# Loading Wv by rows and entering the first two token tiles centred only, in the opening of a four-layer kernel

## Chip, cores, metric

One core of one Trainium2 chip. The metric is the device time of one execution in microseconds (us), median of several executions. The kernel before took 1295.47 us (3 runs, 1295.15 to 1295.88).

## The reference

The input is 2048 tokens of 1024 channels in bf16. Two kinds of layer alternate, twice each: dilated local attention, and an MLP that mixes tokens. Only the entry of the first attention layer matters here.

```python
x = x + A(layernorm(x), wqkv, wo)         # A: q, k, v = h @ wqkv ; local attention ; @ wo
x = x + B(layernorm(x), w1, b1, w2, b2)   # B: MLP over tokens
x = x + A(layernorm(x), wqkv, wo)
x = x + B(layernorm(x), w1, b1, w2, b2)
```

Layernorm is (x - mean) * rs with rs = 1 / sqrt(var + eps), one mean and one rs per token. The text calls the computation of rs the rsqrt; the kernel makes it of two small ScalarE operations, Ln and Exp. V is layernorm(x) @ Wv, and Wv is the last third of the columns of wqkv.

## The kernel before

Tokens come in 16 tiles of 128. In the opening each tile is loaded, gets its statistics and rs, is normalized and then transposed into hT, because the matmul wants channels on the partitions. Tiles 0 to 4 are transposed on TensorE into PSUM, the memory that holds matmul results, and copied to hT by ScalarE; the rest go by DMA transposes. To evict a result is to copy it out of PSUM, so that its buffer is free again. V of a tile is two output halves (n = 0, 1) of 512 columns, each a sum of eight matmuls over the eight blocks kt of 128 channels. Each engine works through a list of its own in the order written:

```python
def w_load(n, hf):      # 512 KB: one half of the columns of four kt, so rows of 1 KB
    return nc.sync.dma_start(out=wv[n][hf][:], in_=wq_v[:, hf*4:(hf+1)*4, 2*D + n*512:2*D + (n+1)*512])
def R_(k):  ...         # ScalarE: rs = Exp(-0.5 * Ln(var + eps))
def N_(k, hs): ...      # VectorE: x = (x - mean) * rs
def tr(k): ...          # TensorE: eight 128x128 transposes into PSUM
def C_(k, hf): ...      # ScalarE: four of them to hT
def V_(k, n, kts): ...  # TensorE: matmuls of tile k, half n, blocks kts
def E_(k, n):           # ScalarE: evict the finished half to v
    return nc.scalar.copy(out=v[c][i][:, n*512:(n+1)*512], in_=pss_[k, n][:])

for _ in range(14):     # warm matmuls on zeros, results unused: they are to get the clock fast
    chain_("PE", lambda: nc.tensor.matmul(wm[:], lhsT=warm[:, 0:P], rhs=warm[:], start=True, stop=True))
# ... cut ...
pe = [(tr, 0), (V_, 0, 0, lo4), (tr, 1), (V_, 0, 0, hi4), (V_, 1, 0, lo4), (tr, 2), (V_, 1, 0, hi4),
      (V_, 2, 0, a8), (V_, 0, 1, a8), (tr, 3), (V_, 1, 1, a8), (V_, 2, 1, a8), (tr, 4)]
pe += [(V_, k, n, a8) for k in range(3, NT) for n in range(NDC)]
act = [(R_, 0), (C_, 0, 0), (R_, 1), (C_, 0, 1), (C_, 1, 0), (C_, 1, 1), (R_, 2), (E_, 0, 0), (C_, 2, 0), (C_, 2, 1),
       (E_, 1, 0), (R_, 3), (E_, 2, 0), (R_, 4), (E_, 0, 1), (C_, 3, 0), ...]   # cut
```

The warm matmuls are there because the matmul clock starts slow: in this profile 512-column matmuls are issued every 0.427 us up to 7.3 us and every 0.216 us after that.

The softmax here doesn't subtract the row's maximum and nothing guards it: scores larger than these inputs give would overflow.

Of the kernel before, what the change touches and what calls it, by code (L numbers as in the profile page):

```python
# [14 lines left out]
P = 128  # L15
# [10 lines left out]
def kernel(  # L26
# [85 lines left out]
    def ln_exp_table():  # L112
        return tc.keep_in_program_order(nc.scalar.preload_act_table_set("natural_log_exp_and_others"))

    ln_exp_table()
    ident = const.tile([P, P], BF16, name="ident")
    make_identity(nc, ident[:])
    eps1 = const.tile([P, 1], FP32, name="eps1")
# [9 lines left out]
    for r in range(P // KG):  # L128
        hb_ = band[r * KG:(r + 1) * KG]
        nc.gpsimd.affine_select(out=hb_, in_=hb_, compare_op=ALU.is_ge, fill=0.0, base=0,  # L130
                                pattern=[[1, GW]], channel_multiplier=-1)
        nc.gpsimd.affine_select(out=hb_, in_=hb_, compare_op=ALU.is_ge, fill=0.0, base=W - 1,
                                pattern=[[-1, GW]], channel_multiplier=1)
    b1_bf = const.tile([P, FT], BF16, name="b1_bf")
    b2_bf = const.tile([P, NI, DIL], BF16, name="b2_bf")
    b1_sb = const.tile([P, FT], FP32, name="b1_sb")
# [48 lines left out]
        return mv[:, 0:1], rs  # L185

    def norm_dve(dst, x, mean, rs):
        return nc.vector.tensor_scalar(out=dst, in0=x, scalar1=mean, scalar2=rs[:], op0=ALU.subtract, op1=ALU.mult)

    def norm_act(dst, x, mean, rs):  # L190
        bi = st("bi", [P, 1])
# [11 lines left out]

    def start_up(v, wv):
        np_ = 5
        warm = x2("warm", [P, 512])
        nc.vector.memset(warm[:], 0.0)
        xs, tps, pss_, mvs, sts, rss = {}, {}, {}, {}, {}, {}

        def x_load(k, hs=(slice(0, D),)):  # L210
            c, i = order[k]
            if k % 2 == 0:
                x_load.t = gop.tile([P, GF, D], BF16, name="x0", tag="go")
            xs[k] = x_load.t[:, k % 2, :]
            for h in hs:
                r = nc.sync.dma_start(out=xs[k][:, h], in_=xin_v[c, i][:, h])
            return r

        def w_load(n, hf):
            return nc.sync.dma_start(out=wv[n][hf][:], in_=wq_v[:, hf * (KD // 2):(hf + 1) * (KD // 2),  # L220
                                                                2 * D + n * 512:2 * D + (n + 1) * 512])

        def S_(k, cc):
            if cc == 0:
                sts[k] = st("bn", [P, NDC, 6])
            return nc.vector.bn_stats(out=sts[k][:, cc, :], in_=xs[k][:, cc * 512:(cc + 1) * 512])

        def A_(k):
            mvs[k] = st("mv", [P, 2])
            return nc.vector.bn_aggr(out=mvs[k][:], in_=sts[k][:])  # L230

        def R_(k):
            rss[k] = st("rs", [P, 1])
            return rsqrt(rss[k][:], mvs[k][:, 1:2], 1.0, eps1)

        def N_(k, hs):
            for h in hs:
                r = norm_dve(xs[k][:, h], xs[k][:, h], mvs[k][:, 0:1], rss[k])
            return r

        def tr(k):
            tps[k] = pss.tile([P, KD, P], BF16, name="s", tag="s")
            for kt in range(KD):
                r = nc.tensor.transpose(tps[k][:, kt, :], xs[k][:, kt * P:(kt + 1) * P], ident[:])
            return r

        def C_(k, hf):
            ks = slice(hf * KD // 2, (hf + 1) * KD // 2)
            return nc.scalar.copy(out=hT[:, ks, cols(*order[k])], in_=tps[k][:, ks, :])  # L249

        def V_(k, n, kts):
            if kts[0] == 0:
                pss_[k, n] = m_tile()
            for kt in kts:
                r = nc.tensor.matmul(pss_[k, n][:], lhsT=hT[:, kt, cols(*order[k])], rhs=wv[n][kt // 4][:, kt % 4, :],  # L255
                                     start=(kt == 0), stop=(kt == KD - 1))
            return r

        def E_(k, n):
            c, i = order[k]  # L260
            return nc.scalar.copy(out=v[c][i][:, n * 512:(n + 1) * 512], in_=pss_[k, n][:])

        def T_(k):
            return nc.sync.dma_start_transpose(out=hT[:, :, cols(*order[k])], in_=xs[k])

        wm = m_tile()
        for _ in range(14):
            chain_("PE", lambda: nc.tensor.matmul(wm[:], lhsT=warm[:, 0:P], rhs=warm[:], start=True, stop=True))  # L268

        halves = (slice(0, D // 2), slice(D // 2, D))  # L270
        whole = (slice(0, D),)
        chain_("SP", x_load, 0, halves)
        chain_("SP", x_load, 1)
        chain_("SP", w_load, 0, 0)
        chain_("SP", x_load, 2)
        chain_("SP", w_load, 0, 1)
        chain_("SP", x_load, 3)
        chain_("SP", w_load, 1, 0)
        chain_("SP", w_load, 1, 1)
        for k in range(4, NT):  # L280
            chain_("SP", x_load, k)

        lo4, hi4 = range(KD // 2), range(KD // 2, KD)
        a8 = range(KD)
        pe = [(tr, 0), (V_, 0, 0, lo4), (tr, 1), (V_, 0, 0, hi4), (V_, 1, 0, lo4), (tr, 2), (V_, 1, 0, hi4),
              (V_, 2, 0, a8), (V_, 0, 1, a8), (tr, 3), (V_, 1, 1, a8), (V_, 2, 1, a8), (tr, 4)]
        pe += [(V_, k, n, a8) for k in range(3, NT) for n in range(NDC)]
        act = [(R_, 0), (C_, 0, 0), (R_, 1), (C_, 0, 1), (C_, 1, 0), (C_, 1, 1), (R_, 2), (E_, 0, 0), (C_, 2, 0), (C_, 2, 1),
               (E_, 1, 0), (R_, 3), (E_, 2, 0), (R_, 4), (E_, 0, 1), (C_, 3, 0), (C_, 3, 1), (R_, 5), (E_, 1, 1), (R_, 6),
               (E_, 2, 1), (C_, 4, 0), (C_, 4, 1)]  # L290
        es = [(E_, k, n) for k in range(3, NT) for n in range(NDC)]
        rs = [(R_, k) for k in range(7, NT)]
        for j, e in enumerate(es):
            act.append(e)
            if rs and j % 4 != 3:
                act.append(rs.pop(0))
        dve = [(S_, 0, 0), (S_, 0, 1), (A_, 0), (S_, 1, 0), (N_, 0, halves), (S_, 1, 1), (A_, 1), (N_, 1, whole),
               (S_, 2, 0), (S_, 2, 1), (A_, 2)]
        for k in range(2, NT):
            nx = k + 1 < NT  # L300
            if nx:
                dve.append((S_, k + 1, 0))
            dve.append((N_, k, whole))
            if nx:
                dve += [(S_, k + 1, 1), (A_, k + 1)]
        dve.append((zero_fill,))
        dve.append((cast_biases,))
        sp = [(T_, k) for k in range(np_, NT)] + [(load_biases,)]
        qs = {"PE": pe, "ACT": act, "DVE": dve, "SP": sp}
        need = {cast_biases: lambda: (load_biases,) in done, R_: lambda k: k in mvs, N_: lambda k, h: k in rss, tr: lambda k: (N_, k) in done, C_: lambda k, hf: k in tps,  # L310
                V_: lambda k, n, kts: ((C_, k, 1 if kts[-1] == KD - 1 else 0) in done or (T_, k) in done), E_: lambda k, n: (V_, k, n) in done,
                T_: lambda k: (N_, k) in done}
        done = set()
        while any(qs.values()):
            for eng, q in qs.items():
                while q and (q[0][0] not in need or need[q[0][0]](*q[0][1:])):
                    f, *args = q.pop(0)
                    chain_(eng, f, *args)
                    if f is V_:
                        if args[2][-1] == KD - 1:  # L320
                            done.add((f, args[0], args[1]))
                    else:
                        done.add((f, *(args if f is C_ else args[:1])))

    def load_wv():
        return [[wt_("wv", [P, KD // 2, 512]) for _ in range(2)] for _ in range(NDC)]

    def fill_wv(wv, n):
        for hf in range(2):
            nc.sync.dma_start(out=wv[n][hf][:],  # L330
                              in_=wq_v[:, hf * (KD // 2):(hf + 1) * (KD // 2), 2 * D + n * 512:2 * D + (n + 1) * 512])

    def v_proj(v, c, i, wv, ns):
        for n in ns:
            ps = m_tile()
            for kt in range(KD):
                nc.tensor.matmul(ps[:], lhsT=hT[:, kt, cols(c, i)], rhs=wv[n][kt // 4][:, kt % 4, :],  # L337
                                 start=(kt == 0), stop=(kt == KD - 1))
            nc.scalar.copy(out=v[c][i][:, n * 512:(n + 1) * 512], in_=ps[:])

# [242 lines left out]
    def gemm2(c, i, w2t, g, src, dst, to_hT):  # L583
# [17 lines left out]
            nc.sync.dma_start(out=dst, in_=xo[:])  # L601
        if to_hT:
            mean, rs = stats(xo, 1.0, eps1)
            norm_dve(xs[:], xo[:], mean, rs)
            nc.sync.dma_start_transpose(out=hT[:, :, cols(c, i)], in_=xs[:])

    NU = NG * DIL
    for li in range(2):
# [8 lines left out]
            chain_("SP", load_qk, 0, wts)  # L617
            res = lambda c, i: xin_v[c, i]
        else:
            fill_wv(wv, 0)  # L620
            fill_wv(wv, 1)
            wts = [None, None]
            chain_("SP", load_qk, 0, wts)
            for i in range(NI):
# [107 lines left out]
```

## Time and profile before

| | kernel before |
|---|---|
| median, 3 runs | 1295.47 us |
| span of the profiled execution | 1293.7 us |
| TensorE busy | 1276.5 us (99%) |
| first transpose of tile 0 | 7.32 us |
| first V matmul of tile 0 | 8.61 us |
| first V matmul of tile 3 | 21.54 us |
| first q matmul (all of V issued) | 66.43 us |

Two lines of the page: each engine's busy time in us, its share of the span and its number of instructions; and the shares of the chain of work that ended last.

```profile
PE 1276.5 (99%) x8286; PEld 593.7 (46%) x8442; DVE 417.3 (32%) x852; ACT 373.2 (29%) x628; POOL 2.4 (0%) x15
...
PE 98%; issue 1%; DVE 0%; DMA 0%; ACT 0%; SPq 0%
```

TensorE bounds everything. The Trainium skill warns ("Perfetto Trace Analysis", its opening note) that busy time of pipelined matmuls says little about distance from the peak. It does here only because the issue times agree: from 21.54 us to the first q matmul, and in the MLP stages, 512-column matmuls are issued every 0.216 us without a break, so this change can move the end only if TensorE reaches that stretch earlier.

The timeline of the opening, TensorE only (start, length, engine, line, operation, number of instructions, and in brackets idle time before and what ended it; a few matmul records are missing from a trace, so that x19 stands for 20). L268 are the warm matmuls, L244 the transposes, L255 the V matmuls:

```profile
1.38 6.11 PE L268 MATMUL m<-warm 128*128 128x512 bf16 x14 [1.38 <-DVE warm L207]
7.32 0.61 PE L244 MATMUL s<-ident,x 128*128 128x128 bf16 x8
8.61 1.04 PE L255 MATMUL m<-wv,hT 128*128 128x512 bf16 x4 [0.68 <-ACT hT L249]
9.62 0.62 PE L244 MATMUL s<-ident,x 128*128 128x128 bf16 x8
10.08 1.89 PE L255 MATMUL m<-wv,hT 128*128 128x512 bf16 x8
12.42 0.62 PE L244 MATMUL s<-ident,x 128*128 128x128 bf16 x8 [0.45 <-DVE x L188]
13.09 4.26 PE L255 MATMUL m<-wv,hT 128*128 128x512 bf16 x19
17.19 0.61 PE L244 MATMUL s<-ident,x 128*128 128x128 bf16 x8
17.64 3.62 PE L255 MATMUL m<-wv,hT 128*128 128x512 bf16 x16
21.09 0.61 PE L244 MATMUL s<-ident,x 128*128 128x128 bf16 x8
```

After tile 0 starts, only the transposes of tile 2 (12.42) are waited for noticeably. From the full timeline, Ln, Exp and the normalization of tile 0:

```profile
4.80 0.29 ACT L174 ACTIVATE ln<-mv,eps 128x1 f32<-128x1 f32 x1 [2.72 <-DVE mv L230]
5.12 0.20 ACT L175 ACTIVATE rs<-ln 128x1 f32<-128x1 f32 x1
5.37 0.73 DVE L188 TENSOR_SCALAR x<-x,mv,rs 128x512 bf16<-128x512 bf16 x2
```

### The profile page before, as it was taken

How to read it: one execution, taken by the hardware profiler on the slowest of the kernel's cores; microseconds unless marked ns; L12 is line 12 of the kernel's file. 1: busy time of each engine (PE TensorE's matmuls, PEld its weight loads, DVE VectorE, ACT ScalarE, POOL GpSimd, SP SyncE). 2: the span in 40 equal slices, each digit the busy share in tenths (PEclk: the TensorE clock that was granted, in tenths of full speed). 3: DMA queues.
4: the chain of work that ended last, by engine and by line, in shares of the span. 5: the costliest groups of instructions: out<-in, count | busy, mean ns of one | idle time of the engine just before them, and what ended most of it. 6: DMA issues, size and time to landing. Idle time of an engine off the chain costs nothing.

```text
span 1293.7 us, 19400 instructions
## 1 busy us (share of the span) xinstructions
PE 1276.5 (99%) x8286; PEld 593.7 (46%) x8442; DVE 417.3 (32%) x852; ACT 373.2 (29%) x628; POOL 2.4 (0%) x15
## 2 busy tenths in 40 slices
PE   9999999999999999999999999999999999999999
PEld 4444444444444444444444444444444444444444
DVE  7457767830000022322300667778100000111111
ACT  5456665541111100000023666644311111000000
POOL 0000000000000000000000000000000000000000
PEclk9999999999999999999999999999999999999999
DMA  7411123643222135456510111246422222334331
GB/s 236 82 44 48 51 80 122 204 138 90 65 78 80 57 101 148 124 155 147 130 33 1 46 51 49 80 151 209 125 66 86 78 59 78 105 106 135 118 92 33
DMA packets 201862, 125.54 MB, mean 97 GB/s; under 512 B 39984, under 2 KB 183600, under 8 KB 201776
## 3 DMA queue, kind: packets, MB, share of 16 engines
q1 hardware_dynamic: 201776, 124.30, 33.9%
q8 instruction: 66, 1.08, 0.3%
q14 instruction: 20, 0.16, 0.0%
HBM read 96.48 MB, written 16.78 MB: 88 GB/s over the span
## 4 chain that ended last, share of the span: by engine, by line
PE 98%; issue 1%; DVE 0%; DMA 0%; ACT 0%; SPq 0%
PE m L352 17%; PE s L594 15%; PE s L547 15%; PE m L467 8%; PE acc L547 7%; PE m L547 7%; PE acc L594 7%; PE m L594 7%; PE m L337 4%; PE m L255 4%; PE s L383 2%; PE acc L418 1%; PE acc L422 1%; PE m L268 0%; DMA qB<-qs 0%
## 5 line engine op out<-in xcount | busy, mean ns | idle before, releaser
L594 PEld LDWEIGHTS <-w 128*128 128x128 bf16 x1820 | 177.0, 98 | 210.2
L547 PEld LDWEIGHTS <-w 128*128 128x128 bf16 x1792 | 175.4, 98 | 211.4
L352 PE MATMUL m<-hT,wqk 128*128 128x512 bf16 x963 | 223.3, 379 | 6.2 <-issue 4.6
L547 PE MATMUL s<-h,w 128*128 128x512 bf16 x878 | 201.2, 379 | 0.8
L594 PE MATMUL s<-g,w 128*128 128x512 bf16 (+1 forms) x912 | 201.0, 374 | 0.7
L596 DVE SCALAR_TENSOR_TENSOR xo<-s,b_sb,xs 128x512 bf16<-128x512 f32 (+1 forms) x33 | 24.4, 739 | 532.9 <-PE s L594 527.6
L352 PEld LDWEIGHTS <-wqk 128*128 128x128 bf16 x1024 | 95.3, 98 | 117.9 <-issue 10.7
L398 DVE TENSOR_TENSOR Pm<-pc,band 32x640 bf16<-32x640 bf16 x256 | 123.5, 483 | 66.0 <-ACT pc L386 56.6
L467 PE MATMUL m<-wo,oT 128*128 128x512 bf16 x500 | 110.6, 379 | 0.8 <-issue 0.3
L547 PE MATMUL acc<-h,w 128*128 128x512 bf16 x440 | 103.1, 379 | 0.5
L594 PE MATMUL acc<-g,w 128*128 128x512 bf16 x436 | 99.7, 379 | 0.5
L547 PE MATMUL m<-h,w 128*128 128x512 bf16 x438 | 98.5, 379 | 0.5
L594 PE MATMUL m<-g,w 128*128 128x512 bf16 (+1 forms) x436 | 96.9, 376 | 0.6
L174 ACT ACTIVATE ln<-mv,eps 128x1 f32<-128x1 f32 x64 | 18.9, 295 | 221.1 <-DVE mv L182 184.9
L467 PEld LDWEIGHTS <-oT 128*128 128x128 bf16 x512 | 49.6, 98 | 60.3 <-issue 1.3
L554 ACT ACTIVATE g<-s,b_sb 128x1024 bf16<-128x1024 f32 x28 | 31.2, 1114 | 158.2 <-PE s L547 146.5
L363 DVE COPY qB<-qs 32x512 bf16<-32x512 bf16 x136 | 38.1, 280 | 90.5 <-ACT qs L359 89.2
L255 PE MATMUL m<-wv,hT 128*128 128x512 bf16 x250 | 55.6, 379 | 1.0 <-ACT hT L249 0.7
L337 PE MATMUL m<-wv,hT 128*128 128x512 bf16 x251 | 55.2, 379 | 0.3
L386 ACT ACTIVATE pc<-s,shift 128x640 bf16<-128x640 f32 x64 | 51.2, 800 | 12.2 <-PE s L383 12.1
L359 ACT CAST qs<-m 128x512 bf16<-128x512 f32 x64 | 37.5, 586 | 49.1 <-PE m L352 48.0
L356 ACT CAST kT<-m 128x512 bf16<-128x512 f32 x64 | 37.5, 586 | 46.4 <-PE m L352 46.4
(58 smaller groups left out, 675.1 us busy)
## 6 DMA issues: line engine op xcount, KB each, us to landing
w<-in_B_w_dram SPq DMA_DIRECT2D x56, 512.0 KB, 3.8
w<-in_B_w_dram SPq DMA_DIRECT2D x64, 448.0 KB, 4.5
wqk<-in_A_wqkv_dram SPq DMA_DIRECT2D x16, 512.0 KB, 4.8
xa<-xn SPq DMA_DIRECT2D x32, 256.0 KB, 2.2
xs<-xa SPq DMA_DIRECT2D x32, 256.0 KB, 3.1
wv<-in_A_wqkv_dram SPq DMA_DIRECT2D x8, 512.0 KB, 5.7
wo<-in_A_wo_dram SPq DMA_DIRECT2D x8, 512.0 KB, 6.0
xr<-in_A_x_dram SPq DMA_DIRECT2D x16, 256.0 KB, 3.3
```

Source lines behind the costliest of these rows:

```text
L255: r = nc.tensor.matmul(pss_[k, n][:], lhsT=hT[:, kt, cols(*order[k])], rhs=wv[n][kt // 4][:, kt % 4, :], start=(kt == 0), stop=(kt == KD - 1))
L337: nc.tensor.matmul(ps[:], lhsT=hT[:, kt, cols(c, i)], rhs=wv[n][kt // 4][:, kt % 4, :], start=(kt == 0), stop=(kt == KD - 1))
L352: mm = nc.tensor.matmul(ps[:], lhsT=wts[part][:, kt, (g % 2) * P:(g % 2 + 1) * P], rhs=hT[:, kt, lo:lo + 512], start=(kt == 0), stop=(kt = ...
L356: nc.scalar.copy(out=kT[u % 2][:, ls], in_=ps[:])
L359: nc.scalar.copy(out=qs[:], in_=ps[:])
L363: nc.vector.tensor_copy(out=qB[u % 2][hp, h, ls], in_=qs[hp, :])
L386: nc.scalar.activation(out=pc[:].rearrange("p (n t) h k -> p n (t h k)", n=2), in_=ss[:, :, 0:2 * HG * GW], func=ACT.Exp, scale=scale, bia ...
L398: mm = nc.vector.tensor_tensor(out=Pm[rp, :, s0:s0 + HB, r * KG:r * KG + GW].rearrange("p h t k -> p t h k"), in0=pc[rp], in1=mk, op=ALU.mult)
L467: mm = nc.tensor.matmul(ps[:], lhsT=oT[g][:, cols(c, i)], rhs=wo[n][g // 4][:, g % 4, :], start=(g == 0), stop=(g == NG - 1))
L547: nc.tensor.matmul(pairs[fl][0][dc], lhsT=wt[c][:, i, fl * P:(fl + 1) * P], rhs=h2[c][i][:, dc * 512:(dc + 1) * 512], start=(k == 0), stop ...
L554: nc.scalar.activation(out=g[fb][:, fl, :].rearrange("p (n d) -> p n d", n=2), in_=t[:], func=ACT.Gelu_apprx_tanh, bias=b1_sb[:, ft:ft + 1])
L594: nc.tensor.matmul(ap, lhsT=w2t[ft // HF][:, ft % HF, c::DIL], rhs=g[ft // GF][:, ft % GF, lo:lo + w], start=(ft == 0), stop=(ft == FT - 1))
```

## The change

The intent: reach V sooner. Tiles 0 and 1 enter hT centred only (x - mean), so they need not wait for rs; rs is applied when V is evicted. Wv comes as eight chunks of 256 KB with full 2 KB rows, and each chunk serves both output halves of both tiles. Because q and k need the normalized tiles, tiles 0 and 1 are normalized and DMA-transposed into hT a second time later. There are 10 warm matmuls, then 2 more behind the first transposes. The core of the diff, the rest cut:

```diff
-        def w_load(n, hf):
-            return nc.sync.dma_start(out=wv[n][hf][:], in_=wq_v[:, hf * (KD // 2):(hf + 1) * (KD // 2),
-                                                                2 * D + n * 512:2 * D + (n + 1) * 512])
+        def w_load(kt):
+            return nc.sync.dma_start(out=wv[kt // 2][:, kt % 2, :], in_=wq_v[:, kt, 2 * D:3 * D])
+        def M_(k, h):     # VectorE: centre
+            return nc.vector.tensor_scalar(out=xc[k][:, h], in0=xs[k][:, h], scalar1=mvs[k][:, 0:1], scalar2=None,
+                                           op0=ALU.subtract)
+        def Ma(k, h):     # ScalarE: centre
+            return nc.scalar.activation(out=xc[k][:, h], in_=xs[k][:, h], func=ACT.Identity, bias=nm0[:])
 # E_:
+            if k < 2:
+                return nc.scalar.activation(out=dst, in_=src, func=ACT.Identity, scale=rss[k])
-        for _ in range(14):
+        for _ in range(10):
 # loads: Wv 0 to 3, x of tile 2, Wv 4 and 5, x of tile 3, Wv 6 and 7
+        pe = [(tr, 0), (W_, 2), *VV(0, 0, 1), (tr, 1), *VV(0, 2), *VV(1, 0, 1, 2)]
+        for kt in range(3, 6):
+            pe += [*VV(0, kt), *VV(1, kt)]
+        pe += [(tr, 2), *VV(0, 6, 7), *VV(1, 6, 7), (V_, 2, 0, a8), (tr, 3), (V_, 2, 1, a8), (tr, 4)]
+        act = [(Ma, 0, halves[1]), (C_, 0, 0), (C_, 0, 1), (R_, 0), (C_, 1, 0), (C_, 1, 1), (R_, 1), (R_, 2), (C_, 2, 0), (C_, 2, 1),
+               (E_, 0, 0), (E_, 0, 1), (E_, 1, 0), (E_, 1, 1), (R_, 3), (R_, 4), (C_, 3, 0), (C_, 3, 1), (E_, 2, 0),
+               (R_, 5), (C_, 4, 0), (C_, 4, 1), (E_, 2, 1), (R_, 6)]
+            if k in (8, 9):
+                dve.append((N_, k - 8, whole))
-        sp = [(T_, k) for k in range(np_, NT)] + [(load_biases,)]
+        sp = [(T_, k) for k in (*range(np_, NT), 0, 1)] + [(load_biases,)]
```

VV(k, kt) is one matmul of tile k for each output half. In the second attention layer Wv is also loaded by rows; nothing else there changes.

More of the change, by code (lines that the diff above doesn't have):

```diff
@@ L113, in ln_exp_table @@
         return tc.keep_in_program_order(nc.scalar.preload_act_table_set("natural_log_exp_and_others"))
-    ln_exp_table()
     ident = const.tile([P, P], BF16, name="ident")
@@ L133 @@
                                 pattern=[[-1, GW]], channel_multiplier=1)
+    mv01 = const.tile([P, 2, 2], FP32, name="mv01")
+    rs01 = const.tile([P, 2], FP32, name="rs01")
+    nm0 = const.tile([P, 1], FP32, name="nm0")
     b1_bf = const.tile([P, FT], BF16, name="b1_bf")
@@ L187, in norm_dve @@
     def norm_dve(dst, x, mean, rs):
-        return nc.vector.tensor_scalar(out=dst, in0=x, scalar1=mean, scalar2=rs[:], op0=ALU.subtract, op1=ALU.mult)
+        return nc.vector.tensor_scalar(out=dst, in0=x, scalar1=mean, scalar2=rs, op0=ALU.subtract, op1=ALU.mult)
     def norm_act(dst, x, mean, rs):
@@ L205, in start_up @@
         np_ = 5
+        xc = [x2(f"xc{k}") for k in range(2)]
         warm = x2("warm", [P, 512])
@@ L228, in A_, with B_ @@
         def A_(k):
-            mvs[k] = st("mv", [P, 2])
-            return nc.vector.bn_aggr(out=mvs[k][:], in_=sts[k][:])
+            mvs[k] = mv01[:, k, :] if k < 2 else st("mv", [P, 2])[:]
+            return nc.vector.bn_aggr(out=mvs[k], in_=sts[k][:])
+        def B_(k):
+            return nc.vector.tensor_scalar(out=nm0[:], in0=mvs[k][:, 0:1], scalar1=-1.0, scalar2=None, op0=ALU.mult)
+        def M_(k, h):
[3 more added lines that the diff above has]
+            return nc.scalar.activation(out=xc[k][:, h], in_=xs[k][:, h], func=ACT.Identity, bias=nm0[:])
         def R_(k):
-            rss[k] = st("rs", [P, 1])
-            return rsqrt(rss[k][:], mvs[k][:, 1:2], 1.0, eps1)
+            rss[k] = rs01[:, k:k + 1] if k < 2 else st("rs", [P, 1])[:]
+            return rsqrt(rss[k], mvs[k][:, 1:2], 1.0, eps1)
         def N_(k, hs):
@@ L243, in tr @@
             for kt in range(KD):
-                r = nc.tensor.transpose(tps[k][:, kt, :], xs[k][:, kt * P:(kt + 1) * P], ident[:])
+                r = nc.tensor.transpose(tps[k][:, kt, :], (xc[k] if k < 2 else xs[k])[:, kt * P:(kt + 1) * P], ident[:])
             return r
@@ L251, in V_ @@
         def V_(k, n, kts):
-            if kts[0] == 0:
-                pss_[k, n] = m_tile()
+            if kts[0] == 0 and k == 1:
+                if n == 0:
+                    V_.t = a_tile()
+                pss_[k, n] = V_.t[:, n, :]
+            elif kts[0] == 0:
+                pss_[k, n] = m_tile()[:]
             for kt in kts:
-                r = nc.tensor.matmul(pss_[k, n][:], lhsT=hT[:, kt, cols(*order[k])], rhs=wv[n][kt // 4][:, kt % 4, :],
+                r = nc.tensor.matmul(pss_[k, n], lhsT=hT[:, kt, cols(*order[k])], rhs=wv[kt // 2][:, kt % 2, n * 512:(n + 1) * 512],
                                      start=(kt == 0), stop=(kt == KD - 1))
@@ L260, in E_ @@
             c, i = order[k]
-            return nc.scalar.copy(out=v[c][i][:, n * 512:(n + 1) * 512], in_=pss_[k, n][:])
+            dst, src = v[c][i][:, n * 512:(n + 1) * 512], pss_[k, n]
+            if k < 2:
+                return nc.scalar.activation(out=dst, in_=src, func=ACT.Identity, scale=rss[k])
+            return nc.scalar.copy(out=dst, in_=src)
         def T_(k):
             return nc.sync.dma_start_transpose(out=hT[:, :, cols(*order[k])], in_=xs[k])
-        wm = m_tile()
-        for _ in range(14):
-            chain_("PE", lambda: nc.tensor.matmul(wm[:], lhsT=warm[:, 0:P], rhs=warm[:], start=True, stop=True))
+        wm = s_tile()
@@ L270, in start_up, with W_ @@
+        def W_(n):
+            for _ in range(n):
+                r = nc.tensor.matmul(wm[:, 0, :], lhsT=warm[:, 0:P], rhs=warm[:], start=True, stop=True)
+            return r
+        for _ in range(10):
+            chain_("PE", W_, 1)
         halves = (slice(0, D // 2), slice(D // 2, D))
         whole = (slice(0, D),)
+        chain_("ACT", ln_exp_table)
         chain_("SP", x_load, 0, halves)
         chain_("SP", x_load, 1)
-        chain_("SP", w_load, 0, 0)
+        for kt in range(4):
+            chain_("SP", w_load, kt)
@@ L275, in start_up, with VV @@
         chain_("SP", x_load, 2)
-        chain_("SP", w_load, 0, 1)
+        chain_("SP", w_load, 4)
+        chain_("SP", w_load, 5)
         chain_("SP", x_load, 3)
-        chain_("SP", w_load, 1, 0)
-        chain_("SP", w_load, 1, 1)
+        chain_("SP", w_load, 6)
+        chain_("SP", w_load, 7)
         for k in range(4, NT):
             chain_("SP", x_load, k)
-        lo4, hi4 = range(KD // 2), range(KD // 2, KD)
+        def VV(k, *kts):
+            return [(V_, k, n, [kt]) for kt in kts for n in range(NDC)]
@@ L284, in start_up @@
         a8 = range(KD)
-        pe = [(tr, 0), (V_, 0, 0, lo4), (tr, 1), (V_, 0, 0, hi4), (V_, 1, 0, lo4), (tr, 2), (V_, 1, 0, hi4),
-              (V_, 2, 0, a8), (V_, 0, 1, a8), (tr, 3), (V_, 1, 1, a8), (V_, 2, 1, a8), (tr, 4)]
+        pe = [(tr, 0), (W_, 2), *VV(0, 0, 1), (tr, 1), *VV(0, 2), *VV(1, 0, 1, 2)]
+        for kt in range(3, 6):
+            pe += [*VV(0, kt), *VV(1, kt)]
+        pe += [(tr, 2), *VV(0, 6, 7), *VV(1, 6, 7), (V_, 2, 0, a8), (tr, 3), (V_, 2, 1, a8), (tr, 4)]
         pe += [(V_, k, n, a8) for k in range(3, NT) for n in range(NDC)]
-        act = [(R_, 0), (C_, 0, 0), (R_, 1), (C_, 0, 1), (C_, 1, 0), (C_, 1, 1), (R_, 2), (E_, 0, 0), (C_, 2, 0), (C_, 2, 1),
-               (E_, 1, 0), (R_, 3), (E_, 2, 0), (R_, 4), (E_, 0, 1), (C_, 3, 0), (C_, 3, 1), (R_, 5), (E_, 1, 1), (R_, 6),
-               (E_, 2, 1), (C_, 4, 0), (C_, 4, 1)]
+        act = [(Ma, 0, halves[1]), (C_, 0, 0), (C_, 0, 1), (R_, 0), (C_, 1, 0), (C_, 1, 1), (R_, 1), (R_, 2), (C_, 2, 0), (C_, 2, 1),
+               (E_, 0, 0), (E_, 0, 1), (E_, 1, 0), (E_, 1, 1), (R_, 3), (R_, 4), (C_, 3, 0), (C_, 3, 1), (E_, 2, 0),
+               (R_, 5), (C_, 4, 0), (C_, 4, 1), (E_, 2, 1), (R_, 6)]
@@ L296, in start_up @@
                 act.append(rs.pop(0))
-        dve = [(S_, 0, 0), (S_, 0, 1), (A_, 0), (S_, 1, 0), (N_, 0, halves), (S_, 1, 1), (A_, 1), (N_, 1, whole),
+        dve = [(S_, 0, 0), (S_, 0, 1), (A_, 0), (B_, 0), (M_, 0, halves[0]), (S_, 1, 0), (S_, 1, 1), (A_, 1), (M_, 1, whole[0]),
                (S_, 2, 0), (S_, 2, 1), (A_, 2)]
@@ L305, in start_up @@
                 dve += [(S_, k + 1, 1), (A_, k + 1)]
+            if k in (8, 9):
+                dve.append((N_, k - 8, whole))
         dve.append((zero_fill,))
         dve.append((cast_biases,))
-        sp = [(T_, k) for k in range(np_, NT)] + [(load_biases,)]
+        sp = [(T_, k) for k in (*range(np_, NT), 0, 1)] + [(load_biases,)]
         qs = {"PE": pe, "ACT": act, "DVE": dve, "SP": sp}
-        need = {cast_biases: lambda: (load_biases,) in done, R_: lambda k: k in mvs, N_: lambda k, h: k in rss, tr: lambda k: (N_, k) in done, C_: lambda k, hf: k in tps,
-                V_: lambda k, n, kts: ((C_, k, 1 if kts[-1] == KD - 1 else 0) in done or (T_, k) in done), E_: lambda k, n: (V_, k, n) in done,
-                T_: lambda k: (N_, k) in done}
+        need = {cast_biases: lambda: (load_biases,) in done, R_: lambda k: k in mvs, N_: lambda k, h: k in rss, tr: lambda k: (N_, k) in done if k > 1 else (M_, k) in done and (k == 1 or (Ma, k) in done),
+                B_: lambda k: k in mvs, M_: lambda k, h: k in mvs, Ma: lambda k, h: (B_, k) in done, C_: lambda k, hf: k in tps,
+                V_: lambda k, n, kts: ((C_, k, kts[-1] * 2 // KD) in done or (T_, k) in done), E_: lambda k, n: (V_, k, n) in done and k in rss,
+                T_: lambda k: (N_, k) in done and (k > 1 or (E_, k, 1) in done)}
         done = set()
@@ L322, in start_up, with fill_wv @@
                     else:
-                        done.add((f, *(args if f is C_ else args[:1])))
+                        done.add((f, *(args if f in (C_, E_) else args[:1])))
     def load_wv():
-        return [[wt_("wv", [P, KD // 2, 512]) for _ in range(2)] for _ in range(NDC)]
-    def fill_wv(wv, n):
-        for hf in range(2):
-            nc.sync.dma_start(out=wv[n][hf][:],
-                              in_=wq_v[:, hf * (KD // 2):(hf + 1) * (KD // 2), 2 * D + n * 512:2 * D + (n + 1) * 512])
+        return [wt_("wv", [P, 2, D]) for _ in range(KD // 2)]
+    def fill_wv(wv):
+        for j in range(KD // 2):
+            nc.sync.dma_start(out=wv[j][:], in_=wq_v[:, 2 * j:2 * j + 2, 2 * D:3 * D])
     def v_proj(v, c, i, wv, ns):
@@ L336, in v_proj @@
             for kt in range(KD):
-                nc.tensor.matmul(ps[:], lhsT=hT[:, kt, cols(c, i)], rhs=wv[n][kt // 4][:, kt % 4, :],
+                nc.tensor.matmul(ps[:], lhsT=hT[:, kt, cols(c, i)], rhs=wv[kt // 2][:, kt % 2, n * 512:(n + 1) * 512],
                                  start=(kt == 0), stop=(kt == KD - 1))
@@ L603, in gemm2 @@
             mean, rs = stats(xo, 1.0, eps1)
-            norm_dve(xs[:], xo[:], mean, rs)
+            norm_dve(xs[:], xo[:], mean, rs[:])
             nc.sync.dma_start_transpose(out=hT[:, :, cols(c, i)], in_=xs[:])
@@ L619 @@
         else:
-            fill_wv(wv, 0)
-            fill_wv(wv, 1)
+            fill_wv(wv)
             wts = [None, None]
```

## The prediction

> **What bounds the kernel.** TensorE. The busy table gives PE 1276.5 of 1293.7 us; the chain that ended last is 98% PE. After 21.5 us the matmuls run back to back at 0.216 us to the end, so the change acts only through the time at which PE reaches that stretch: in the timeline, the first V matmul of tile 3 at 21.54 us. Before it PE does 14 warm matmuls, then from 7.32 us 13.4 us of needed work (40 transposes, 48 matmuls) with gaps of 0.7 (first copy to hT), 0.3 and 0.45 to 0.8 us (normalized tile 2). At most some 2 us of gaps plus an earlier start are to be won.
>
> **What the change does, with the timeline's durations.**
> - The first transposes no longer wait for Ln and Exp (0.29 + 0.20) and two normalizing halves (0.73). The aggregate ends at 4.77; the centring halves run in parallel on DVE (0.37) and ACT (0.59), to about 5.6. Ten warm matmuls end at 1.38 + 10 x 0.427 = 5.65: transposes start near 5.65, not 7.32.
> - The clock is then still cold: matmuls are 0.427 apart until 7.32, 0.216 after. The Trainium skill, "TensorE: Matmul & The Clock Gate", Part 1, says about 3.4 us of sustained activity, judged in a free-running window, warms it; the trace shows 5.9 us. Eight cold transposes (0.85 estimated) and two warm matmuls (0.85) bring V of tile 0 to 7.4, not 8.61.
> - Wv: with queues full, a 512 KB chunk of 1 KB rows took 1.49 us, 256 KB of 2 KB rows 0.67. The eight chunks should land between 5.9 and 12.4 us, ahead of use. ("DMA: Bandwidth & Descriptors", Specifications, puts line rate at 512 B and up; the trace shows 12% between 1 and 2 KB.) PE didn't wait for weights and won't.
> - Tile 1's copy costs about 0.4 us of wait; transposes of tile 2 come near 13.4.
> - Given back: ACT now does two copies, then four evictions of tiles 0 and 1 in a row (0.48 each, issue to issue) before the rsqrt of tile 3. I estimate that rsqrt at 17.0, its normalize at 17.5, transposes at 18.1, while PE finishes V of tile 2, first half, at 17.4: 0.7 us idle. The rsqrt of tile 4 waits in turn for DVE (18.9); its transposes end near 20.7, then two waits of 0.3 for evictions. V of tile 3 starts near 21.0; at V of tile 4 the gain is about 0.2 us.
> - Two normalizations (0.55 each) and two DMA transposes (2 us each) are added behind; q/k weights are issued 4 us later (about 52.5, landing near 58.5). PE needs them at 66.4: no cost.
> - Second layer: Wv lands 15 us before use. Nothing.
>
> So 1.2 us gained at the start are nearly all given back on ACT before tile 4.
>
> **Predicted time** 1295.2 us, 8 in 10 between 1294.2 and 1296.2. Faster by over 2%: 0.01; within 2%: 0.98; slower: 0.01.
>
> **What would show it.** Timeline: transposes of tile 0 at 5.6 to 5.8; V of tile 0 at 7.2 to 7.6; no PE wait for wv; PE idle 0.5 to 1.2 us before the transposes of tile 3, released by its normalize; V of tile 3 at 20.5 to 21.5; first q matmul at 66.0 to 66.6 (66.4 before).
>
> **What would make it wrong.** The clock warming earlier or later (0.5 us either way); ACT overlapping better, so that tile 3 is not late (gain up to 1.5 us); wv chunks landing late (loss of 1 us); the last transposes landing after 66 us (loss of some us).

## The result, and the profile after

| | before | after |
|---|---|---|
| median of 6 runs, same rounds | 1295.28 us | 1295.82 us |
| lowest to highest | 1294.65 to 1295.88 | 1294.93 to 1296.29 |
| ratio, 95% interval | | 1.0004 (0.9991 to 1.0017) |
| first transpose of tile 0 (one profile each) | 7.32 us | 5.62 us |
| first V matmul of tile 0 | 8.61 us | 7.36 us |
| first V matmul of tile 3 | 21.54 us | 21.37 us |
| first q matmul | 66.43 us | 66.61 us |
| from V of tile 0 to first q, "the stretch" | 57.82 us | 59.25 us |

A ratio is the mean time of one kernel's runs over that of the other's runs of the same rounds, so it is not quite the ratio of the medians.

The time did not move. The same two lines of the page, after:

```profile
PE 1276.2 (99%) x8284; PEld 593.7 (46%) x8440; DVE 417.8 (32%) x854; ACT 373.5 (29%) x629; POOL 2.4 (0%) x15
...
PE 97%; issue 1%; ACT 1%; DVE 0%; DMA 0%; SPq 0%
```

ScalarE has entered the chain with 1%. Where, the timeline of TensorE says (L289 warm matmuls, L256 transposes, L271 V):

```profile
1.38 4.45 PE L289 MATMUL s<-warm 128*128 128x512 bf16 x10 [1.38 <-DVE warm L210]
5.62 1.06 PE L256 MATMUL s<-ident,xc 128*128 128x128 bf16 x8
6.48 0.77 PE L289 MATMUL s<-warm 128*128 128x512 bf16 x2
7.36 1.04 PE L271 MATMUL m<-wv,hT 128*128 128x512 bf16 x4
8.23 0.61 PE L256 MATMUL s<-ident,xc 128*128 128x128 bf16 x8
8.68 0.59 PE L271 MATMUL m<-wv,hT 128*128 128x512 bf16 x2
9.52 1.47 PE L271 MATMUL acc<-wv,hT 128*128 128x512 bf16 x6 [0.25 <-ACT hT L261]
...
13.42 0.61 PE L256 MATMUL s<-ident,x 128*128 128x128 bf16 x8
...
15.78 1.89 PE L271 MATMUL m<-wv,hT 128*128 128x512 bf16 x8
18.52 0.62 PE L256 MATMUL s<-ident,x 128*128 128x128 bf16 x8 [0.85 <-DVE x L190]
18.97 1.89 PE L271 MATMUL m<-wv,hT 128*128 128x512 bf16 x8
20.70 0.61 PE L256 MATMUL s<-ident,x 128*128 128x128 bf16 x8
21.37 5.82 PE L271 MATMUL m<-wv,hT 128*128 128x512 bf16 x24
```

The head start of 1.25 us (8.61 - 7.36) is there. What V of tile 0 waited for is not printed, but ScalarE's line shows it (two copies, of which the first ends near 7.31):

```profile
6.72 1.07 ACT L261 COPY hT<-s 128x512 bf16<-128x512 bf16 x2 [1.05 <-PE s L256]
```

Further on, tile 2 is transposed at 13.42, with most of V of tiles 0 and 1 done. Then TensorE stops before the transposes of tile 3 (18.52). Issue to issue it is 1.01 us without work: the last matmul before them was issued at 17.29 and the next could have gone out 0.216 us later. Summed from the issue times, the gaps between V of tile 0 and V of tile 4 are 2.10 us after and 0.75 us before; the 1.35 us between them are nearly all of the 1.43 us by which the stretch grew.

The bracket names the normalization of tile 3 on VectorE as what ended the wait. That was waiting in turn. From the full timeline of the changed kernel, ScalarE (L261 copies to hT, L279 scaled evictions, L176 and L177 Ln and Exp) and VectorE (L190):

```profile
14.06 1.07 ACT L261 COPY hT<-s 128x512 bf16<-128x512 bf16 x2 [2.32 <-PE s L256]
15.03 1.28 ACT L279 ACTIVATE v<-m,rs 128x512 bf16<-128x512 f32 x2
16.18 1.29 ACT L279 ACTIVATE v<-acc,rs 128x512 bf16<-128x512 f32 x2
17.32 0.33 ACT L176 ACTIVATE ln<-mv,eps 128x1 f32<-128x1 f32 x1
17.68 0.20 ACT L177 ACTIVATE rs<-ln 128x1 f32<-128x1 f32 x1
17.91 0.55 DVE L190 TENSOR_SCALAR x<-x,mv,rs 128x1024 bf16<-128x1024 bf16 x1 [3.63 <-ACT rs L177]
```

The statistics of tile 3 were ready at 13.56 us, while ScalarE had been idle for 2.32 us until 14.06. Its list, however, puts six large operations before the rsqrt of tile 3, so that came at 17.32 and VectorE idled for 3.63 us.

### The profile page after: what moved, and what is told of

It reads as the page before. It is cut to its first block, busy times and chain, and to the rows that moved or that the text cites. A ratio compares the mean times of both kernels' runs of the same rounds, so it can differ in the third digit from the quotient of the medians.

```text
span 1293.7 us, 19408 instructions
## 1 busy us (share of the span) xinstructions
PE 1276.2 (99%) x8284; PEld 593.7 (46%) x8440; DVE 417.8 (32%) x854; ACT 373.5 (29%) x629; POOL 2.4 (0%) x15
## 3 DMA queue, kind: packets, MB, share of 16 engines
q8 instruction: 66, 1.08, 0.4%
## 4 chain that ended last, share of the span: by engine, by line
PE 97%; issue 1%; ACT 1%; DVE 0%; DMA 0%; SPq 0%
PE m L386 17%; PE s L628 15%; PE s L581 15%; PE m L501 8%; PE acc L581 7%; PE m L581 7%; PE acc L628 7%; PE m L628 7%; PE m L371 4%; PE m L271 4%; PE s L417 2%; PE acc L452 1%; PE acc L456 1%; PE s L289 0%; ACT hT L261 0%
## 5 line engine op out<-in xcount | busy, mean ns | idle before, releaser
L176 ACT ACTIVATE ln<-mv,eps 128x1 f32<-128x1 f32 x64 | 18.9, 296 | 224.1 <-DVE mv L184 184.9
L371 PE MATMUL m<-wv,hT 128*128 128x512 bf16 x251 | 55.2, 379 | 0.3
L271 PE MATMUL m<-wv,hT 128*128 128x512 bf16 x234 | 53.0, 379 | 0.6
```

The costliest lines, as they stand in the source:

```text
L271: r = nc.tensor.matmul(pss_[k, n], lhsT=hT[:, kt, cols(*order[k])], rhs=wv[kt // 2][:, kt % 2, n * 512:(n + 1) * 512], start=(kt == 0), st ...
L371: nc.tensor.matmul(ps[:], lhsT=hT[:, kt, cols(c, i)], rhs=wv[kt // 2][:, kt % 2, n * 512:(n + 1) * 512], start=(kt == 0), stop=(kt == KD - 1))
```

## The experiments

Theory A: the head start is real and is lost on ScalarE, because the rsqrt of tile 3 stands behind the evictions of tiles 0 and 1. Rival B: it is lost because x of tiles 2 and 3 lands later behind the Wv chunks (9.62 and 11.54 us, against 7.75 and 10.01). Rival C: the second entry of tiles 0 and 1 costs time. Theory D, on the head start itself: before, the start was held by the 14 warm matmuls, and centring is worth little.

The executions differ by 1 to 2 us for reasons shown below, as much as is at stake. So each kernel is judged first by its trace: the stretch from V of tile 0 to the first q matmul. All runs, with the moment at which the matmul clock turned fast (from an issue spacing of 0.427 to 0.216 us, worked out from the spacing of the matmul during which it turned):

| kernel | clock fast at, us | V tile 0 | first q | stretch | median, us | ratio to before, interval |
|---|---|---|---|---|---|---|
| before | 7.3 | 8.61 | 66.43 | 57.82 | 1295.28 | 1 |
| before, again | 6.1 | 8.03 | 65.85 | 57.82 | 1295.29 | 0.9999 (0.9985 to 1.0012) |
| after | 6.8 | 7.36 | 66.61 | 59.25 | 1295.82 | 1.0004 (0.9991 to 1.0017) |
| after, again | 7.3 | 7.36 | 66.60 | 59.24 | 1295.64 | 1.0001 (0.9989 to 1.0014) |
| e1 rsqrt first | 5.2 | 6.79 | 64.58 | 57.80 | 1293.44 | 0.9994 (0.9981 to 1.0006) |
| e2 evict twice | 5.5 | 6.83 | 67.22 | 60.39 | 1297.21 | 1.0020 (1.0007 to 1.0032) |
| e3 normalized | 7.3 | 7.85 | 66.87 | 59.02 | 1296.20 | 1.0005 (0.9993 to 1.0018) |
| e4 no gaps | 5.9 | 7.03 | 64.08 | 57.05 | 1292.98 | 0.9988 (0.9975 to 1.0000) |
| e4 again | 5.5 | 6.86 | 64.48 | 57.63 | 1293.75 | 0.9984 (0.9972 to 0.9997) |
| e5 before, 11 warm | 5.2 | 7.26 | 65.36 | 58.10 | 1293.89 | 0.9996 (0.9982 to 1.0009) |
| e6 no re-entry | 6.7 | 7.36 | 66.60 | 59.24 | 1296.21 | 1.0003 (0.9990 to 1.0017) |
| e7 x early | 4.6 | 6.80 | 66.04 | 59.24 | 1295.72 | 1.0000 (0.9988 to 1.0013) |
| e8 no warm | 9.9 | 7.02 | 67.52 | 60.50 | 1297.02 | 1.0009 (0.9997 to 1.0022) |
| e9 both on VectorE | 6.8 | 6.93 | 64.04 | 57.10 | 1293.05 | 0.9981 (0.9969 to 0.9994) |

Read it by the columns: chance moves V of tile 0 through the clock, the program nearly fixes the stretch. The four at 59.24 to 59.25, which have the same orders on TensorE and ScalarE, repeat it to 0.01 us with the clock turning anywhere between 4.6 and 7.3, and so do the two of the kernel before. Two rows don't fit this: e4, whose two profiles differ by 0.58 us (see there), and e8, where the clock turned after V of tile 0 had begun. Kernels are compared only within the same rounds. Medians compare only with the kernel before: 1294.52 for e1, e2, e4, e5; 1295.50 for "after, again", e3, e6, e7; 1296.26 for "before, again", "e4 again", e8, e9. The first two rows of the kernel before are its first timing and a later one.

### The yardstick repeated

> The changed kernel unaltered, as the yardstick of this call and for a second profile. All theories: within 0.15% of the kernel before. In the timeline the stretch from the first V matmul of tile 0 to the first q matmul is 59.25 us again (57.82 in the kernel before), whatever the moment at which the clock turns fast.

It came out so: stretch 59.24 us, ratio 1.0001.

### e1: rsqrt of tiles 3 and 4 ahead of the evictions

```diff
-        ... (R_, 1), (R_, 2), (C_, 2, 0), (C_, 2, 1),
-               (E_, 0, 0), (E_, 0, 1), (E_, 1, 0), (E_, 1, 1), (R_, 3), (R_, 4), (C_, 3, 0), ...
+        ... (R_, 1), (R_, 2), (R_, 3), (C_, 2, 0), (C_, 2, 1),
+               (E_, 0, 0), (R_, 4), (E_, 0, 1), (E_, 1, 0), (E_, 1, 1), (C_, 3, 0), ...
```

> Changed kernel with only the ScalarE order of the opening altered: the rsqrt (Ln, Exp) of tile 3 goes before the two copies of tile 2, that of tile 4 after the first eviction, instead of both behind the four scaled evictions of tiles 0 and 1. Theory A (the head start is lost because tile 3's rsqrt queues behind the evictions on ScalarE): no PE wait for the normalize of tile 3 (0.8 to 1.0 us in the changed kernel), V of tile 3 at about 20.2 us (21.4), first q matmul at 65.0 to 65.5 us (66.6), time about 1.3 us below the changed kernel. Rival B (tiles 2 and 3 of x land later because the weight rows go first): the wait before the transposes of tile 3 stays, time as the changed kernel. Rival C (entering tiles 0 and 1 a second time costs time behind the opening): PE gets ahead in the opening but the first q matmul stays at 66.6.

The timeline of TensorE:

```profile
15.26 1.89 PE L271 MATMUL m<-wv,hT 128*128 128x512 bf16 x8
16.98 0.61 PE L256 MATMUL s<-ident,x 128*128 128x128 bf16 x8
17.43 1.89 PE L271 MATMUL m<-wv,hT 128*128 128x512 bf16 x8
19.16 0.61 PE L256 MATMUL s<-ident,x 128*128 128x128 bf16 x8
19.61 7.59 PE L271 MATMUL m<-wv,hT 128*128 128x512 bf16 x33
```

The wait before tile 3 is gone: from 15.26 on there is no idle time in brackets. The stretch fell from 59.25 to 57.80 us, which is that of the kernel before. The rest of the way to 64.58 is the clock, which turned 1.6 us earlier in this execution and put V of tile 0 at 6.79. Only the order of a list changed, so theory A holds (two entries moved together, those of tiles 3 and 4; of the 1.45 us regained, 1.01 is the wait before tile 3); the loads of x and the second entry were as in the changed kernel, so B and C have nothing left to explain. The median is 1.08 us below that of the kernel before of the same rounds, but the interval still includes no change.

### e2: the suspected cost enlarged

```diff
-               (E_, 0, 0), (E_, 0, 1), (E_, 1, 0), (E_, 1, 1), (R_, 3), (R_, 4), ...
+               (E_, 0, 0), (E_, 0, 1), (E_, 1, 0), (E_, 1, 1), (E_, 1, 0), (E_, 1, 1), (R_, 3), (R_, 4), ...
```

> Changed kernel with the two scaled evictions of tile 1 made twice, ahead of the rsqrt of tile 3 (same values, 1.14 us more on ScalarE at that place). Theory A: the wait of PE before the transposes of tile 3 grows from 1.0 to about 2.1 us, first q matmul at about 67.8 us (66.6), time about 1.1 us above the changed kernel. Rivals B and C: the two extra evictions hide in ScalarE's idle time, no change.

The waits of TensorE in the first 70 us (who waited for whom: us in total, times, longest):

```profile
PE s L256 <- DVE x L190: 2.0, 1, 2.0
PE s L289 <- DVE warm L210: 1.4, 1, 1.4
```

In the changed kernel the first of these lines has 0.8. The stretch grew by 1.14 us, to 60.39: exactly two scaled evictions of 0.57 us. The first q matmul was at 67.22, not 67.8, because V of tile 0 came 0.53 us earlier with the clock. This is the one experiment whose interval lies wholly above that of no change (1.0020). What stands before that rsqrt goes into the time one to one.

### e3: rows of Wv without centring

Tiles 0 and 1 enter normalized as in the kernel before, with plain evictions and no second entry; 11 warm matmuls ahead; loads of Wv and TensorE's order as in the changed kernel.

```diff
-        dve = [(S_, 0, 0), (S_, 0, 1), (A_, 0), (B_, 0), (M_, 0, halves[0]), (S_, 1, 0), (S_, 1, 1), (A_, 1), (M_, 1, whole[0]),
+        dve = [(S_, 0, 0), (S_, 0, 1), (A_, 0), (S_, 1, 0), (N_, 0, halves), (S_, 1, 1), (A_, 1), (N_, 1, whole),
-        act = [(Ma, 0, halves[1]), (C_, 0, 0), (C_, 0, 1), (R_, 0), (C_, 1, 0), (C_, 1, 1), (R_, 1), (R_, 2),
+        act = [(R_, 0), (C_, 0, 0), (R_, 1), (C_, 0, 1), (C_, 1, 0), (C_, 1, 1), (R_, 2),
```

> The changed kernel without centring: tiles 0 and 1 enter normalized as before, are evicted by plain copies and need no second entry; 11 warm matmuls ahead of them; rows of Wv and the order of the rest kept. Theory D (centring is worth only the time from 5.6 to 6.1 us): transposes of tile 0 at 5.9 to 6.2 us, V of tile 0 at most 0.6 us later than in the changed kernel at the same clock; the stretch from V of tile 0 to the first q matmul 0.2 to 0.4 us shorter than 59.25 (plain evictions at 0.48 us in place of 0.57), time within 0.5 us of the changed kernel. Rival (centring is what buys the head start): 1.2 us or more above it.

```profile
6.14 1.03 PE L255 MATMUL s<-ident,x 128*128 128x128 bf16 x8
7.85 1.04 PE L270 MATMUL m<-wv,hT 128*128 128x512 bf16 x4
```

Transposes of tile 0 at 6.14 us, V of tile 0 at 7.85, 0.49 us later than in "after, again", where the clock turned at the same moment (7.3). The stretch is 0.23 us shorter, so the first q matmul is only 0.26 us later. Centring with all that it brings is worth about a quarter of a microsecond here. The median is 0.56 us above that of "after, again", a little more than I allowed, and inside the noise.

### e4: all gaps closed

```diff
-        pe = [(tr, 0), (W_, 2), *VV(0, 0, 1), (tr, 1), *VV(0, 2), *VV(1, 0, 1, 2)]
-        for kt in range(3, 6):
+        pe = [(tr, 0), (W_, 2), *VV(0, 0, 1), (tr, 1), *VV(0, 2, 3), *VV(1, 0, 1, 2, 3)]
+        for kt in range(4, 6):
-        ... (R_, 2), (C_, 2, 0), (C_, 2, 1),
-               (E_, 0, 0), (E_, 0, 1), (E_, 1, 0), (E_, 1, 1), (R_, 3), (R_, 4), (C_, 3, 0), (C_, 3, 1), (E_, 2, 0),
-               (R_, 5), (C_, 4, 0), (C_, 4, 1), (E_, 2, 1), (R_, 6)]
+        ... (R_, 2), (R_, 3), (C_, 2, 0), (E_, 0, 0), (C_, 2, 1),
+               (R_, 4), (E_, 0, 1), (E_, 1, 0), (E_, 1, 1), (C_, 3, 0), (C_, 3, 1), (E_, 2, 0),
+               (R_, 5), (E_, 2, 1), (C_, 4, 0), (C_, 4, 1), (R_, 6)]
```

> The order of the first experiment, and the rest of the gaps closed: tile 0 uses Wv rows 2 and 3 before tile 1 starts (0.4 us wait for tile 1's copy filled), the first eviction goes between the two copies of tile 2, the second eviction of tile 2 before the copies of tile 4. Theory A: V of tile 3 at about 19.7 us, first q matmul at 64.6 to 65.1 us, time about 1.8 us below the changed kernel and 1.3 to 1.6 below the kernel before (0.1%). Rivals B and C: within 0.5 us of the changed kernel.

> The kernel with the gaps closed, again on another chip. Stretch 57.05 us, V of tile 0 at 6.8 to 7.4 us, first q matmul at 63.9 to 64.4, time 1.0 to 2.0 us below the kernel before (0.08 to 0.15%).

The stretch is 57.05 us the first time. The second time it is 57.63, and the waits show why:

```profile
PE m L271 <- ACT hT L261: 0.2, 1, 0.2
PE m L271 <- DMA wv<-in_A_wqkv_dram: 0.2, 1, 0.2
```

TensorE now runs so close to the loads that it waits for a chunk of Wv (the fourth, issue to issue 0.32 us), which it did in neither profile of the changed kernel. And tile 3 of x landed at 11.52 us, not 11.00 (both have one cause: from the second chunk on, all that stood in the DMA queue landed about 0.5 us later than the first time); its rsqrt, now in front, held the first eviction back on ScalarE, and V of tile 2 started 0.23 us later for want of a PSUM buffer. (The line above names the copy to hT. But the copy that these matmuls need had ended at 14.57, and the eviction that frees one of the two buffers ended at 15.16; V of tile 2 started at 15.21.) The two make up 0.55 of the 0.58 us. I had expected 57.05 again; that part of the expectation failed, and this one profile suggests that the late landing of rival B, harmless in the changed kernel, is what comes next once its queue is in order. The time is below that of the kernel before on both chips, by 0.12% (the interval ends at 1.0000) and 0.16%.

### e5: the kernel before with three warm matmuls fewer

```diff
-        for _ in range(14):
+        for _ in range(11):
```

> The kernel before with 11 warm matmuls in place of 14, nothing else. Theory D (the start before was held by the 14 warm matmuls, which ended at 7.32 us, not by the normalization of tile 0, which ended at 6.10, so most of the head start was there for the taking): transposes of tile 0 at about 6.1 us (7.32), V of tile 0 at 7.9 to 8.3 (cold transposes take 0.4 us longer; 8.61 before), V of tile 3 at about 20.7 to 21.0 (21.54), first q matmul 0.5 to 0.8 us earlier, time 0.5 to 0.8 us below the kernel before. Rival (the warm matmuls are needed for the clock): the clock turns fast later than 7.3 us, and V of tile 3 comes at 21.5 us or later.

```profile
1.38 4.43 PE L268 MATMUL m<-warm 128*128 128x512 bf16 x11 [1.38 <-DVE warm L207]
5.86 0.72 PE L244 MATMUL s<-ident,x 128*128 128x128 bf16 x8
7.26 1.04 PE L255 MATMUL m<-wv,hT 128*128 128x512 bf16 x4 [0.68 <-ACT hT L249]
...
9.30 1.89 PE L255 MATMUL m<-wv,hT 128*128 128x512 bf16 x8 [0.41 <-DMA wv<-in_A_wqkv_dram]
```

Transposes at 5.86, V of tile 0 at 7.26, first q matmul at 65.36: earlier than in either profile of the kernel before, and earlier than in the changed kernel. The clock turned early in this execution, at 5.2 us, so part of this is chance, and the time (0.9996) is not distinguishable from no change. The clock alone would not have given all of the head start. An estimate from the issue spacings, had the clock turned as early with 14 warm matmuls: nine at 0.427 and five at 0.216 us from 1.38 us on end at 6.3, and V of tile 0 follows the first transpose after 1.29 us in both profiles of the kernel before, so at 7.6. This one number is then worth about 0.3 us at V of tile 0 with an early clock (with a late one it was not measured). Hardly any of it reached the q matmuls: TensorE now waited for the second 512 KB chunk of Wv, which landed at 9.26 us, the stretch grew by 0.28 us to 58.10, and the estimate for 14 warm matmuls, 7.6 + 57.82 = 65.4, is what was measured. So theory D holds for the start, but by this estimate fewer warm matmuls alone did not bring the q matmuls forward. That the smaller chunks of Wv are what makes an early start usable fits this, and fits e1 (no wait for Wv with V of tile 0 at 6.79), but no run tests it by itself.

### e6: without the second entry

Wrong on purpose: q and k of tiles 0 and 1 see tiles that are only centred. The two extra normalizations and the two extra DMA transposes are left out.

```diff
-            if k in (8, 9):
-                dve.append((N_, k - 8, whole))
-        sp = [(T_, k) for k in (*range(np_, NT), 0, 1)] + [(load_biases,)]
+        sp = [(T_, k) for k in range(np_, NT)] + [(load_biases,)]
```

> The changed kernel without the second entry of tiles 0 and 1 (their two normalizations and two DMA transposes left out, so q and k of these tiles are wrong on purpose). Theory A: no change, stretch from V of tile 0 to the first q matmul 59.1 to 59.4 us, time within 0.4 us of the changed kernel, q/k weights land about 3 us earlier than 56.6 us, all unused slack. Rival C (the second entry costs): stretch about 58 us, time about 1 us below.

Stretch 59.24 us, first q matmul 66.60. The q/k weights land at 54.4 instead of 56.6 us, and nobody is waiting for them. Rival C falls. The median is 0.57 us above "after, again" where I allowed 0.4. The traces put most of that in the two attention stages (0.9 us more than in "after, again"), which this edit does not touch (see below).

### e7: x of tiles 2 and 3 earlier

```diff
-        for kt in range(4):
+        for kt in range(3):
             chain_("SP", w_load, kt)
         chain_("SP", x_load, 2)
+        chain_("SP", w_load, 3)
+        chain_("SP", x_load, 3)
         chain_("SP", w_load, 4)
         chain_("SP", w_load, 5)
-        chain_("SP", x_load, 3)
```

> The changed kernel with the loads of x for tiles 2 and 3 moved ahead by one and two chunks of Wv. Theory A: tile 2 lands near 9.0 us (9.62), tile 3 near 10.3 (11.54), but the rsqrt of tile 3 still stands behind the evictions on ScalarE: PE waits 0.8 to 1.0 us for its normalize as before, stretch 59.1 to 59.4 us, time within 0.4 us of the changed kernel. Rival B (late landing of x causes the loss): that wait shrinks by over half, time 0.6 us or more below.

Tile 2 landed at 8.13 us and tile 3 at 9.77, even earlier than expected, tile 3 ahead of the kernel before. The wait stayed:

```profile
PE s L256 <- DVE x L190: 0.8, 1, 0.8
```

The stretch is 59.24 us again. Rival B falls.

### The kernel before again, and e8: no warm matmuls

> The kernel before, unaltered, for a second profile. If the clock turns fast at a moment that differs between executions, and its 14 warm matmuls hold the start, then V of tile 0 comes anywhere from 7.4 us (clock fast by 5 us, normalization of tile 0 done at 6.1) to 8.6 us (fast at 7.3), and the stretch from there to the first q matmul is 57.8 to 58.3 us. If the clock always turns at 7.3 us in this kernel, V of tile 0 is at 8.6 again.

```profile
1.38 5.52 PE L268 MATMUL m<-warm 128*128 128x512 bf16 x14 [1.38 <-DVE warm L207]
6.74 0.61 PE L244 MATMUL s<-ident,x 128*128 128x128 bf16 x8
8.03 1.04 PE L255 MATMUL m<-wv,hT 128*128 128x512 bf16 x4 [0.68 <-ACT hT L249]
```

The same 14 warm matmuls took 5.52 us instead of 6.11, because the clock turned at 6.1 us, and V of tile 0 came 0.58 us earlier than in the first profile. The stretch was 57.82 us again. So the head start of the changed kernel is not one number: 1.25 us between the first two profiles, 0.67 between the two "again" profiles (8.03 - 7.36), while the loss is 1.42 or 1.43 in both. The medians of the changed kernel, 0.5 us higher in one set of rounds and 0.1 in the other, lie within the noise and cannot test this.

> The changed kernel without any warm matmul. Transposes of tile 0 start at 5.2 to 5.7 us, cold; V of tile 0 at about 7.4 us as in the changed kernel, but its matmuls are 0.43 us apart until the clock turns, which I expect between 9 and 13 us[...]. Each matmul before that costs 0.21 us more; part is hidden in the waits. First q matmul 0.7 to 3 us later than 66.6, time 0.7 to 3 us above the changed kernel. If the warm matmuls do nothing, first q matmul at 66.6.

All warm matmuls are removed from the changed kernel (10 in front, 2 behind the first transposes).

```profile
5.24 1.10 PE L256 MATMUL s<-ident,xc 128*128 128x128 bf16 x8 [5.24 <-DVE xc L238]
7.02 1.89 PE L271 MATMUL m<-wv,hT 128*128 128x512 bf16 x4 [0.68 <-ACT hT L261]
```

Four matmuls take 1.89 us where the changed kernel needs 1.04. The clock turned at 9.9 us, 4.6 us after the first transpose. The first q matmul came at 67.52 us, 0.9 us later than in the changed kernel, and the stretch was 60.50. So by the trace the warm matmuls are worth having; the median shows no clear difference (1.0009, 0.9997 to 1.0022). e5 and e8 together suggest that their number must fit the arrival of the data.

### e9: both centring halves on VectorE

```diff
 # against e4
-        for _ in range(10):
+        for _ in range(9):
-        ... (A_, 0), (B_, 0), (M_, 0, halves[0]), (S_, 1, 0), ...
+        ... (A_, 0), (M_, 0, halves[0]), (M_, 0, halves[1]), (S_, 1, 0), ...
-        act = [(Ma, 0, halves[1]), (C_, 0, 0), ...
+        act = [(C_, 0, 0), ...
```

> The kernel with the gaps closed, with both centring halves of tile 0 on VectorE (0.34 us each; ScalarE took 0.72 for its half) and 9 warm matmuls ahead. Transposes of tile 0 at 5.2, V of tile 0 at 6.4 to 7.0 us; stretch 57.1 to 57.8 us, as the fourth chunk of Wv (landed at 8.3 to 9.3 us) may now be waited for; first q matmul 63.6 to 64.3 us, time within 0.5 us of the kernel with the gaps closed.

Transposes of tile 0 at 5.19, V of tile 0 at 6.93 (with the clock turning only at 6.8), stretch 57.10, first q matmul 64.04 us. The ratio to the kernel before is 0.9981 (0.9969 to 0.9994). This is the best kernel by its ratio, by 0.2%, and the difference from e4 is within the noise.

### Where the noise comes from

The 14 profiles, cut at the first matmul of each stage, tell how long each stage took from one matmul to the next. Both W1 stages and the first W2 stage (193.39 us each) and the second V stage (55.25 us) repeat to 0.01 us. The two attention stages, from the first q matmul to the first W1 matmul, vary from 197.2 to 198.1 us each, in no order that follows the edits. Together with the clock of the opening this is the spread of an execution: the kernel before alone ranged from 1294.22 to 1296.77 us in nine runs on one chip. What varies inside the attention stages I did not find out. One small part does follow the program: from the last matmul to the end of the span it is 2.91 to 2.92 us in the two profiles of the kernel before and in e5, but 3.05 to 3.09 in the changed kernels and 3.24 in e3 and e6. Why is open; it adds 0.13 to 0.33 us outside the opening.

## Why the prediction was right

The time, 1295.82 us against 1295.2 predicted, lay inside the range, and "within 2%" was certain from the start. Hitting the range proves little: it is 2 us wide, as wide as the executions of either kernel spread, and holds a faster and a slower outcome alike. What was at stake was the mechanism, and in the main it held:

- **Only the opening matters.** Shown but for the 0.13 us after the last matmul: the later V, W1 and W2 stages repeat, the attention stages vary without regard to the edits, and the second layer's Wv by rows changed nothing.
- **Start.** Predicted transposes at 5.65 and V of tile 0 at 7.4 us, measured 5.62 and 7.36. The second hit is partly luck. The sum had V wait for two slow warm matmuls; in the first profile the clock turned at 6.8 us in the midst of them, and V still came at 7.36, because the copy of tile 0 to hT ended near 7.31. The prediction left that copy out, and it took as long.
- **Wv in time.** Chunks predicted between 5.9 and 12.4 us landed from 5.97 to 12.88, and TensorE never waited for one. Two in a row came 0.65 us apart, as estimated (0.67).
- **Tile 1's copy.** 0.4 us predicted, 0.41 measured; transposes of tile 2 predicted at 13.4, measured 13.42.
- **Given back on ScalarE.** Shown by e1 (undone: 1.45 us back), e2 (enlarged: one to one), and by the failure of B (e7) and C (e6).
- **A mis-sized term.** I took 0.48 us from issue to issue for the evictions of tiles 0 and 1, the value of plain copies. Scaled by rs they took 0.57. Four of them put the rsqrt of tile 3 at 17.32, not 17.0, its transposes at 18.5, not 18.1, and the wait at 1.0 us, not 0.7. So the gain of 0.2 us at the end of the opening became a loss of 0.17 in the first pair of profiles (0.75 in the second, by the clock), and the first q matmul came at 66.61 (66.60), the very edge of what I had named. The q/k weights came later by about 2.3 us, not 4, without effect.
- **What I had read wrongly.** The prediction ascribes the earlier start to the waiting for Ln, Exp and the normalization. The profile before already said otherwise: the normalization ended at 6.10 and the last warm matmul held TensorE until 7.32. e3 shows that centring moves V of tile 0 by 0.49 us. The kernel before, e3 and "after, again" all had the clock turn at 7.3 us, so the rest of the 1.25 us, 0.76 from 8.61 to e3's 7.85, goes with the smaller number of warm matmuls ahead. It made no difference to the number predicted, but the statement of cause was only half right.

## What to carry to other kernels

When an engine's work is written as one list for several purposes, look at what stands ahead of the small operation on which the next stage depends: here a 0.5 us rsqrt behind four evictions cost all that a rewritten opening had won, and moving two list entries got it back. Ask of work that is there to keep an engine busy whether it is now what everything waits for, because the profile prints no wait for it; and before counting on what it holds back, ask what comes next (in e5 the next chunk of Wv took the gain). Where a change is worth a thousandth, time a stretch of the trace that the change governs, not the whole run.

## What the Trainium skill lacked or had wrong

- "TensorE: Matmul & The Clock Gate", Part 1, says that the turn to the fast clock varies by about 500 ns from run to run, around 4 us of sustained activity. Here, with matmuls nearly back to back from 1.38 us on, it came between 4.6 and 7.3 us, 3.2 to 6.0 us after the first matmul, in 13 profiles. That does not fit the 500 ns. The same section also says, of a free-running window of 3.4 us, that one kernel can show 6, 11 or 14 cold matmuls, and a spread of that size is what is seen here, though the shortest case, 3.2 us, is below one such window. The advice there, not to fit a model to the count, holds for the whole run (V of tile 0 of the kernel before moved by 0.6 us of 1295), but not for a comparison of openings that differ by as much.
- "ScalarE: Activation LUTs", What ACT_TABLE_LOAD costs, gives 93 ns for each per-partition operand. That nearly agrees: evictions scaled by such an operand took 0.70 to 0.71 us on average in the changed kernel, plain ones 0.59, so 0.11 to 0.12 more. For choosing an eviction the issue spacing counts, 0.57 against 0.48 us in a row, 0.09 more. The page has no figure for the copy that the kernel uses.
- "DMA: Bandwidth & Descriptors", Specifications, puts line rate at 512 B and up. With full queues 512 KB in 1 KB rows took 1.50 us (350 GB/s), 256 KB in 2 KB rows 0.65 to 0.68 us (403 to 386 GB/s), so 2 KB rows were still 10 to 15% better. No page that I read says why the fourth chunk of Wv landed 0.7 to 2.2 us after the third in the profiles with 256 KB chunks, where the first three mostly kept 0.65. (It is not what set e4's two profiles apart: there it came 1.28 and 1.27 us after the third, and the second chunk made the difference.)
- No page that I read says that busy work placed to keep the clock fast hides a wait: 14 warm matmuls held a finished tile for 1.2 us in one profile of the kernel before and for 0.3 us in the other (6.47 to 6.74), and the waits showed none.
